# Pairing the small products on TensorE: z of eight units in four PSUM banks, reads behind scores, and placing transfers issued one by one

## The chip, the cores and the metric

The kernel runs on one core of a Trainium2 chip. The metric is the device time of one execution in microseconds (us).

## The reference, cut to what matters

Eight episodes (B = 8) have eight heads (H = 8), 512 tokens (S), 32 memory states (Ns = N) and 64 channels per head (D). Tokens read from states and states read from tokens; both results, joined along the token axis, go through a feed-forward layer with a squared relu.

```
scores  = scale * x @ state^T        a  = softmax(scores)     xread = a @ state
scores2 = scale * state @ x^T        a2 = softmax(scores2)    sread = a2 @ x
y = concat(xread, sread) as 8 * 544 rows of 512 channels
out = relu(y @ w_in)^2 @ w_out       w_in 512 x 2048, w_out 2048 x 512
```

## The kernel before, in words

**Tiling.** The 2048 hidden channels are 16 blocks of 128. A *unit* is one pair of episode and block: 8 x 16 = 128 units over the tokens (512 columns each), and 16 more over the 256 states of all episodes together. `units` (line 518) lists them in order: episode 0 blocks 0 to 3, episode 1 blocks 0 to 7, the rest of episode 0, the rest of episode 1, and then episodes 2 to 7 whole. `first_of[b]` is the number of an episode's first unit: 32 for episode 2, 48 for episode 3 and so on.

**The hidden product without xread.** The kernel doesn't form xread. As a @ state @ w_in = a @ (state @ w_in), it makes z = state @ w_in per episode and block (`z_piece`, lines 137 to 185), for four units at a time: sixteen matmul records of 64 rows x 32 columns, which lie side by side in the array. ScalarE copies z to z_hi, VectorE subtracts to z_lo, and the attention weights are held as a_hi and a_lo. A unit then is, on TensorE: six matmuls of the hidden product (`up`, line 403: z_hi and z_lo with a_hi and a_lo) and twelve of the output product (`down`, lines 442 to 460: w_out and g, each in a high and a low part). Between them, `relu` (line 406) writes r in SBUF, `square` (line 411) multiplies ph by r on VectorE and leaves the result in the PSUM bank ph, and `high` and `low` (lines 94 to 101) split it into g_hi (ScalarE) and g_lo (VectorE). The first four units (PLAIN) do without the split.

**Scores and reads.** `scores` (line 229) is again a product of 64x32 tiles; the softmax over the states (`soft`, lines 264 to 336) runs mostly on VectorE. For sread, e2 is kept and exponentiated, turned by VectorE (`turn2`, line 338), and moved to its place by sixteen DMAs on SyncE's queue (`place`, lines 345 to 352). Then `read` (lines 354 to 363) multiplies on TensorE in tiles of 128x32, `scale` (line 365) applies the sums, and `collect` (line 372) gathers on GpSimd (POOL).

**PSUM.** Of eight banks, four hold the output products (po), two the hidden products (ph, lines 400 and 70), and two form one buffer px, which z pieces, scores, reads and the turned reads share one after another (lines 71, 160, 216, 355).

**What sets the order.** Each step is registered with an engine, an estimated cost and what it needs (`add`, line 633). `Plan.run` (lines 637 to 684) plays them through and puts on each engine, among the steps ready within 0.35 us, the one with the longest remaining chain; the order that comes out is fixed in the program. On TensorE a line (lines 900 to 947) strings up n, then down n-2 and end n-2 (the second part of down), one unit after another. Visits of z, scores and reads are not on that line: the planner puts them where they are ready. A z piece waits for the px buffer and for the units that used the z buffer two chunks back (lines 837 to 839). Up n waits for g_lo of unit n-2, which frees its bank (line 904). The placing of an episode is one step on SyncE with an estimated cost of 6.0 (line 821).

```
def reads(b, px):                                                      # 816
    add(f"place{b}", SP, 6.0, my["place"], [f"late_turn.{b}", *old], LAND)          # 821
    add(f"read{b}", PE, 1.1, my["read"], [f"place{b}", f"xn{b}", *px], 0.5)         # 822
...
at = first_of[b] - (6.5 if b > 1 else 4.5 if b else 100)               # 879
at = first_of[b + 2] - 9.5 if b + 2 < B else first_of[B - 1] + 2.5 + 4 * (b + 2 - B)
```

The steps' calls in the program:

Of the kernel before, what the change touches and what calls it, by code (L numbers as in the profile page):

```python
# [19 lines left out]
def memory_attention_then_relu2_ffn(  # L20
# [116 lines left out]
    def z_piece(b, units, first, plain):  # L137

        my, own = [], []

        def banks():
            if not own:
                own.extend(ps_o.tile([P, S], F32, name=f"pz{g}", tag="po") for g in range(NG))
            return own

        z_banks[b, units[0]] = banks

        def product():
            c, at = divmod(units[0], ZC)
            if at == 0:  # L150
                zt[b, c] = [
                    sb.tile([P, NG, ZC * P], F32R, name=n, bufs=2) for n in ("z_hi", "z_lo")
                ]
            width = len(units) * P
            cols = slice(units[0] * P, units[0] * P + width)
            dst = slice(at * P, at * P + width)
            if first:
                pz = [bank[:, :width] for bank in banks()]
            else:
                both = ps_x.tile([P, NG, S], F32, name="pz", tag="px")  # L160
                pz = [both[:, g, :width] for g in range(NG)]
            for j in range(HG):
                for g in range(NG):
                    rows = slice(g * D, (g + 1) * D)
                    nc.tensor.matmul(  # L165
                        pz[g][j * N:(j + 1) * N], lhsT=state[b][rows, j, :],
                        rhs=wi[rows, j, cols], start=True, stop=True,
                    )
            z_hi, z_lo = zt[b, c]
            if plain:  # L170
                z = z_hi.bitcast(F32)
                my.extend(
                    (lambda g=g: nc.scalar.copy(out=z[:, g, dst], in_=pz[g]), None)
                    for g in range(NG)
                ) if first else my.append(
                    (lambda: nc.scalar.copy(out=z[:, :, dst], in_=both[:, :, :width]), None)
                )
            elif first:
                my.extend(
                    parts_of(z_hi[:, g, dst], z_lo[:, g, dst], pz[g], nc.vector) for g in range(NG)  # L180
                )
            else:
                my.append(parts_of(z_hi[:, :, dst], z_lo[:, :, dst], both[:, :, :width], nc.vector))

        return product, lambda: [h() for h, l in my], lambda: [l() for h, l in my]
# [3 lines left out]
    def attention(b):  # L189
# [155 lines left out]
        def place():  # L345
            my["e"] = sb.tile([P, NG, NT, HG, N], F32, name="e_t", tag="at", bufs=1)
            for j in range(HG):
                for i in range(P // N):
                    nc.sync.dma_start(  # L349
                        out=my["e"][i * N:(i + 1) * N, :, :, j, :],  # L350
                        in_=my["eq"][j * N:(j + 1) * N, :, :, i, :],
                    )

        def read():
            my["pr"] = ps_x.tile([P, NG, S], F32, name="pr", tag="px")
# [31 lines left out]
    def mlp(parts):  # L387

        todo_, gs = [], {}
# [4 lines left out]
        def up(n):  # L394
# [124 lines left out]
    first_of = [units.index((b, 0)) for b in range(B + 1)]  # L519

    sums = {}

    def batch(b, fcs):
        def first(fc):
            c, i = divmod(fc, ZC)
            f = slice(i * P, (i + 1) * P)
            z_hi, z_lo = zt[b, c]
            if b == 0 and fc < PLAIN:
                at = steps_of[b][0]["at"]()
                return [(z_hi[:, g, f].bitcast(F32), at[:, g, :]) for g in range(NG)]  # L530
            a_hi, a_lo = a_of[b]
            return [
                (w[:, g, f], v[:, g, :])
                for w, v in ((z_hi, a_hi), (z_lo, a_hi), (z_hi, a_lo))
                for g in range(NG)
            ]
# [154 lines left out]

    steps_of = [attention(b) for b in range(B)]
# [32 lines left out]
    last_z = {b: f"z{b}.{max(i for i in range(0, NFC, ZC))}.up" for b in range(B)}  # L725
# [45 lines left out]
    def softmax1(b, px):  # L771
# [3 lines left out]
        if b:  # L775
            add(
                f"scores{b}", PE, 1.3, my["scores"],
                [f"xT{b}", f"state{b}"] + (px if b > 1 else ["z0.0.high"]), 0.7,
# [37 lines left out]
    def reads(b, px):  # L816
# [4 lines left out]
        add(f"place{b}", SP, 6.0, my["place"], [f"late_turn.{b}", *old], LAND)  # L821
        add(f"read{b}", PE, 1.1, my["read"], [f"place{b}", f"xn{b}", *px], 0.5)
# [5 lines left out]
        return [f"scale{b}"]  # L828

    chunks, z_ready = [], {}  # L830

    def z_of(b, cover, first, px):
        chunk = b, cover[0] // ZC
        if chunk not in chunks:
            chunks.append(chunk)
        needs = [f"state{b}"] + [have[fc] for fc in cover]
        if len(chunks) > 2:
            ob, oc = chunks[-3]
            needs += [f"up{ob}.{fc}" for fc in range(oc * ZC, (oc + 1) * ZC)]
        alone = first < 2  # L840
        plain = b == 0 and cover[0] < PLAIN
        product, high, low = z_piece(b, cover, alone, plain)
        needs += ["idle2", "z0.0.high"] * (first == 1)
        name, width = f"z{b}.{cover[0]}.", len(cover) * NG * P
        add(name + "up", PE, 0.5 + 0.6 * width / 1024, product, needs + px * (not alone), 0.4)
        add(name + "high", ACT, act(width), high, [name + "up"])
        done = [name + "high"]
        if not plain:
            add(name + "low", DVE, dve(width), low, [name + "high"])
            done += [name + "low"]  # L850
        z_ready.update({(b, fc): done for fc in cover})
        return px if alone else done
# [13 lines left out]
    now = 0  # L866
    for n, (b, fcs) in enumerate(parts):
        i = fcs[0]
        while i <= fcs[-1]:
            width = ZC if n else 1 if i < 2 else 2  # L870
            first = now + i - fcs[0]
            pairs.append((
                first if first >= 2 else first - 2,
                lambda px, b=b, cover=range(i, i + width), first=first: z_of(b, cover, first, px),
            ))
            i += width
        now += len(fcs)
    for b in range(B):
        at = first_of[b] - (6.5 if b > 1 else 4.5 if b else 100)
        pairs.append((at, lambda px, b=b: softmax1(b, px)))  # L880
        at = first_of[b + 2] - 9.5 if b + 2 < B else first_of[B - 1] + 2.5 + 4 * (b + 2 - B)
        pairs.append((at, lambda px, b=b: reads(b, px)))
# [7 lines left out]
    bank_of = steps_of[0][0]["places"], steps_of[1][0]["places"], z_banks[0, 1]  # L890
# [9 lines left out]
    line, rows = None, []  # L900
    for n, (b, fc) in enumerate(units):
        u, width = name_of[n], blocks[segment[n]]["width"]
        product, relu, square, high, low = up(n)
        needs = [f"{'g_low' if n - 2 >= PLAIN else 'square'}{name_of[n - 2]}"] if n >= 2 else []
        if n < PLAIN:
            needs += z_ready[b, fc] + [f"back{b}.{h}" for h in range(chain_of[b])]
            cost = 8 * MM
        elif b < B:
            needs += z_ready[b, fc] + [
                f"{name}{b}.{h}" for name in ("high", "low") for h in range(chain_of[b])  # L910
            ]
            cost = 6 * MM
        else:
            w_high, w_low = weights_of(fc)
            old = [f"up{name_of[n - 2]}"] if fc >= 2 else [
                f"up{cb}.{i}" for cb, cc in chunks[-2 + fc:][:1] for i in range(cc * ZC, cc * ZC + ZC)
            ]
            add(f"w{fc}.high", ACT, act(NCC * P), w_high, old)
            add(f"w{fc}.low", DVE, dve(NCC * P), w_low, [f"w{fc}.high"])
            needs += [f"w{fc}.high", f"w{fc}.low"]  # L920
            needs += [f"reads{i}.{k}" for i in range(NGB) for k in ("high", "low")]
            cost = 12 * 0.12
        add(f"up{u}", PE, cost, product, needs, 0.25, line)
        line = f"up{u}"
        add(f"relu{u}", ACT, act(width), relu, [line] + ([f"square{name_of[n - 1]}"] if n else []))
        on = (ACT, act(width)) if n < NFC else (DVE, dve(width))
        before = [f"end{name_of[n - 2]}"] if n >= 2 else []
# [78 lines left out]
```

## Time and profile before

| What | Before |
|---|---|
| Median of 3 runs | 661.6 us (661.27 to 661.68) |
| Profiled execution | 661.63 us |
| Its span, first to last instruction | 659.8 us |
| TensorE matmul busy | 644.6 us (98%) |
| VectorE busy | 388.1 us (59%) |
| ScalarE busy | 280.1 us (42%) |
| POOL busy | 9.9 us (1%) |
| Mean granted TensorE clock | 0.999 of 2.4 GHz |

The busy times are shares of the span. Matmuls overlap, and their ends are modelled, so TensorE's busy time says that there was always one under way, not how well they fill the array. What one step adds is read from start to start.

### The profile page before, as it was taken

What the parts mean: (1) busy time and instruction counts of PE and PEld (TensorE: products, weight loads), DVE (VectorE), ACT (ScalarE), POOL (GpSimd) and SP (SyncE); (2) the same over time, 40 slices, a digit from 0 to 9 for tenths busy, and PEclk for the clock granted to TensorE, in tenths of its full rate; (3) what the DMA queues carried; (4) which work ended last, traced back from release to release, by engine and by line L of the source; (5) the groups of instructions that cost most, each with busy time, mean ns of one, the idle gap of its engine ahead of it and who ended that gap; (6) DMA issues with size and microseconds to landing.
All of it is one profiled execution on the core that took longest, in us unless ns stands there. A gap on an engine that the chain in (4) does not pass through costs nothing.

```text
span 659.8 us, 9720 instructions
## 1 busy us (share of the span) xinstructions
PE 644.6 (98%) x3844; PEld 488.4 (74%) x3844; DVE 388.1 (59%) x543; ACT 280.1 (42%) x466; POOL 9.9 (1%) x38
## 2 busy tenths in 40 slices
PE   6799999999999999999999999999999999999997
PEld 4247777777787777777777877777777787778896
DVE  6999798477535844385436744395436653443553
ACT  3767674344323533343333433353334433343542
POOL 0000000000000000000000000000000000000000
PEclk9999999999999999999999999999999999999999
DMA  8534653230212011111121011112120115000100
GB/s 318 199 129 140 212 192 135 66 132 14 84 37 81 18 29 64 65 69 31 66 66 64 17 40 44 65 65 34 64 66 0 24 33 137 2 0 1 65 1 32
DMA packets 51581, 47.81 MB, mean 72 GB/s; under 512 B 36048, under 2 KB 39376, under 8 KB 49744
## 3 DMA queue, kind: packets, MB, share of 16 engines
q1 hardware_dynamic: 51248, 47.00, 22.2%
q8 instruction: 30, 0.49, 0.3%
q10 hardware_dynamic: 288, 0.20, 0.1%
q14 instruction: 15, 0.12, 0.1%
HBM read 34.08 MB, written 8.91 MB: 65 GB/s over the span
## 4 chain that ended last, share of the span: by engine, by line
PE 90%; DVE 3%; DMA 3%; SPq 2%; issue 1%; ACT 0%; DVEq 0%
PE po L458 53%; PE ph L403 28%; PE pz L165 4%; DMA wi_raw<-w_in 3%; SPq L349 2%; PE pr L360 1%; PE po L449 1%; PE pst L234 1%; DVE a_lo L99 0%; DVE wi L122 0%; DVE wof L122 0%; DVE wof L128 0%; SPq L205 0%; DVE g_lo L99 0%; SPq L492 0%
## 5 line engine op out<-in xcount | busy, mean ns | idle before, releaser
L458 PE MATMUL po<-wo_hi,g_hi 128*128 128x512 f32 x528 | 207.2, 392 | 0.0
L458 PE MATMUL po<-wo_lo,g_hi 128*128 128x512 f32 x528 | 205.8, 390 | 0.0
L408 ACT ACTIVATE r<-ph 128x512 f32<-128x512 f32 (+1 forms) x144 | 82.6, 574 | 187.5 <-PE ph L403 187.5
L419 DVE TENSOR_TENSOR ph<-ph,r 128x512 f32<-128x512 f32 (+1 forms) x128 | 85.1, 665 | 113.1 <-ACT r L408 112.9
L458 PE MATMUL po<-wo_hi,g_lo 128*128 128x512 f32 x528 | 150.0, 395 | 0.0
L99 DVE TENSOR_TENSOR g_lo<-ph,g_hi 128x512 fp32r<-128x512 f32 (+1 forms) x140 | 91.5, 654 | 89.9 <-PE po L458 76.3
L458 PEld LDWEIGHTS po<-wo_hi,g_lo 128*128 128x128 f32 x528 | 97.3, 188 | 38.5 <-issue 19.3
L458 PEld LDWEIGHTS po<-wo_hi,g_hi 128*128 128x128 f32 x528 | 99.2, 188 | 30.8 <-ACT r L408 8.4
L96 ACT CAST g_hi<-ph 128x512 fp32r<-128x512 f32 (+1 forms) x140 | 78.9, 564 | 91.4 <-PE po L458 77.3
L458 PEld LDWEIGHTS po<-wo_lo,g_hi 128*128 128x128 f32 x528 | 99.2, 188 | 19.9
L403 PE MATMUL ph<-a_hi,z_hi 128*128 128x512 f32 x248 | 78.9, 399 | 1.0 <-DVE g_lo L99 1.0
L403 PE MATMUL ph<-a_lo,z_hi 128*128 128x512 f32 x248 | 76.8, 391 | 0.4 <-DVE a_lo L99 0.4
L403 PE MATMUL ph<-a_hi,z_lo 128*128 128x512 f32 x248 | 76.8, 391 | 0.2 <-DVE z_lo L99 0.2
L99 DVE TENSOR_TENSOR z_lo<-pz,z_hi 128x1024 fp32r<-128x1024 f32 x31 | 37.9, 1223 | 43.6 <-ACT z_hi L96 42.9
L403 PEld LDWEIGHTS ph<-a_hi,z_hi 128*128 128x128 f32 x248 | 45.6, 188 | 12.9 <-DVE g_lo L99 1.8
L403 PEld LDWEIGHTS ph<-a_lo,z_hi 128*128 128x128 f32 x248 | 46.5, 188 | 10.8 <-DVE a_lo L99 0.8
L403 PEld LDWEIGHTS ph<-a_hi,z_lo 128*128 128x128 f32 x248 | 46.5, 188 | 10.4 <-DVE z_lo L99 0.6
L96 ACT CAST z_hi<-pz 128x1024 fp32r<-128x1024 f32 x31 | 31.5, 1015 | 45.7 <-PE pz L165 45.7
L165 PE MATMUL pz<-wi,sp_raw 64*32 64x512 f32 (+2 forms) x544 | 35.3, 576 | 0.0
L375 POOL COPY sr<-rd 32x128 f32<-32x128 f32 x32 | 9.2, 287 | 551.6 <-DVE rd L367 550.5
L165 PEld LDWEIGHTS pz<-wi,sp_raw 64*32 64x32 f32 x544 | 6.3, 105 | 13.0 <-issue 7.2
L113 ACT ACTIVATE wi<-wi_raw 128x1024 f32<-128x1024 f32 (+1 forms) x9 | 9.4, 1040 | 14.0 <-DMA wi_raw<-w_in 14.0
(85 smaller groups left out, 418.8 us busy)
## 6 DMA issues: line engine op xcount, KB each, us to landing
wo_raw<-w_out SPq DMA_DIRECT2D x8, 1024.0 KB, 5.0
xn_raw<-xn SPq DMA_DIRECT2D x8, 1024.0 KB, 5.5
out<-sum SPq DMA_DIRECT2D x32, 256.0 KB, 2.3
xt_raw<-xT SPq DMA_DIRECT2D x7, 1024.0 KB, 5.3
wi_raw<-w_in SPq DMA_DIRECT2D x7, 1024.0 KB, 4.8
e_t<-eq SPq DMA_DIRECT2D x128, 32.0 KB, 1.9
wi_raw<-w_in SPq DMA_DIRECT2D x2, 512.0 KB, 5.7
xt_raw<-xT SPq DMA_DIRECT2D x2, 512.0 KB, 6.0
```

Source lines behind the costliest of these rows:

```text
L96: nc.scalar.copy(out=hi, in_=src)
L99: eng_lo.tensor_sub(out=lo, in0=src, in1=hi.bitcast(F32))
L113: nc.scalar.activation(out_f, high.bitcast(F32), AF.Abs, scale=2.0**-112)
L165: nc.tensor.matmul(pz[g][j * N:(j + 1) * N], lhsT=state[b][rows, j, :], rhs=wi[rows, j, cols], start=True, stop=True,)
L234: nc.tensor.matmul(place[g][j * N:(j + 1) * N], lhsT=state[b][rows, j, :], rhs=my["t"][rows, j, own], start=True, stop=True,)
L349: nc.sync.dma_start(out=my["e"][i * N:(i + 1) * N, :, :, j, :], in_=my["eq"][j * N:(j + 1) * N, :, :, i, :],)
L360: nc.tensor.matmul(my["pr"][j * N:(j + 1) * N, g, :D], lhsT=my["e"][:, g, t, j, :], rhs=my["n"][:, t, h * D:(h + 1) * D], start=t == 0, st ...
L375: nc.gpsimd.tensor_copy(out=sr[b // GB][at:at + N, j * NG * D:(j + 1) * NG * D], in_=my["rd"][j * N:(j + 1) * N].rearrange("p g d -> p (g ...
L403: nc.tensor.matmul(ph, lhsT=w, rhs=v, start=m == 0, stop=m == len(todo) - 1)
L408: nc.scalar.activation(r, my[0], AF.Relu)
L419: nc.vector.tensor_mul(out=ph, in0=ph, in1=r)
L458: nc.tensor.matmul(po[t], lhsT=g, rhs=w, start=i == 0 and j == 0, stop=i == last and j == 2)
```

## The change

**z.** From unit 32 on, a chunk of four units is one of a pair. The pair stands on TensorE's line at a *slot*: ahead of up n-6, if n is the pair's first unit. Its first piece takes the two ph banks (one for each half of the heads, evacuated by two copies and two subtractions), its second the px buffer. In such a slot, down n-2 and end n-2 (n here the slot's unit) come ahead of up n. z is kept as unit by half by column, and half of the z chunks lie in the buffers that had held the raw weights (tag `raw`), so a chunk waits for the units four chunks back, not two.

**Scores and reads.** From episode 2 on, the scores of episode b stand on the line ahead of up `first_of[b] - 10`, and the reads of episode b-2 right behind them. The reads of the last two episodes stand ahead of units 117 and 121. Reads use one ph bank in place of px.

**Relu and square.** From unit 24 on (`kept_from`), r has three buffers and the square is r * r in SBUF. The bank ph is free after the relu; up n waits for the relu of unit n-2. In every unit, whatever stands in the slot takes its bank in the same turn.

**Placing** is sixteen steps of 0.65 in the planner, one for each DMA, in a row but with others between them where the planner sees fit.

The diff, cut:

```diff
+    def z_tiles(k):
+        if k not in zt and in_raw(k):
+            both = sb.tile([P, 2, ZC, NG, P], F32R, name="z_both", tag="raw", bufs=RAW)
+            zt[k] = [both[:, 0], both[:, 1]]
+        if k not in zt:
+            zt[k] = [sb.tile([P, ZC, NG, P], F32R, name=n, bufs=2) for n in ("z_hi", "z_lo")]
+        return zt[k]
...
+            if not own and home == "px":
+                both = ps_x.tile([P, NG, S], F32, name="pz", tag="px")
+                own.extend(both[:, g] for g in range(NG))
+                own.append(both)
+            elif not own:
+                pool = dict(po=ps_o, ph=ps_h)[home]
+                own.extend(pool.tile([P, S], F32, name=f"pz{g}", tag=home) for g in range(NG))
...
-        def place():
-            my["e"] = sb.tile([P, NG, NT, HG, N], F32, name="e_t", tag="at", bufs=1)
-            for j in range(HG):
-                for i in range(P // N):
...
+        def place(k):
+            j, i = divmod(k, P // N)
...
-            my["pr"] = ps_x.tile([P, NG, S], F32, name="pr", tag="px")
+            my["pr"] = ps_h.tile([P, NG, S // NG], F32, name="pr", tag="ph")
...
-                r = sb.tile([P, S], F32, name="r", bufs=1)[:, :width]
+                if n < kept_from or n % 3 == 0:
+                    r = sb.tile([P, S], F32, name="r", bufs=1)[:, :width]
+                else:
+                    if not r_late:
+                        r_late.append(sb.tile([P, 2, S], F32, name="r_late", tag="wof", bufs=1))
+                    r = r_late[0][:, n % 3 - 1, :width]
...
+                if n >= kept_from:
+                    nc.vector.tensor_mul(out=r, in0=r, in1=r)
+                    my[0] = r
+                    return
...
+    late_from = first_of[2]
+    kept_from = late_from - 8
+    def in_raw(k):
+        return k * ZC >= late_from and k % 4 < 2
...
+    pieces = [(0, 1, "po", None), (1, 1, "po", None), (2, 2, "px", None)]
+    pieces += [(n, ZC, "px", None) for n in range(PLAIN, late_from, ZC)]
+    for n in range(late_from, first_of[B], 2 * ZC):
+        pieces += [(n, ZC, "ph", n - 6), (n + ZC, ZC, "px", n - 6)]
...
-                f"scores{b}", PE, 1.3, my["scores"],
+                f"scores{b}", PE, 1.1, my["scores"],
...
+    def in_slot(n, name, free=()):
+        before = slots.setdefault(n, [])
+        line = before[-1][0] if before else f"end{name_of[n - 3]}"
+        before.append((name, free))
+        return line
...
-        add(f"place{b}", SP, 6.0, my["place"], [f"late_turn.{b}", *old], LAND)
-        add(f"read{b}", PE, 1.1, my["read"], [f"place{b}", f"xn{b}", *px], 0.5)
+        for k in range(HG * P // N):
+            add(
+                f"place{b}.{k}", SP, 0.65, lambda k=k: my["place"](k),
+                [f"late_turn.{b}", *old], LAND, f"place{b}.{k - 1}" if k else None,
+            )
...
+            f"read{b}", PE, 0.9, my["read"], [f"place{b}", f"xn{b}"], 0.3,
+            in_slot(slot, f"read{b}", [[f"scale{b}"]]),
...
-        add(name + "up", PE, 0.5 + 0.6 * width / 1024, product, needs + px * (not alone), 0.4)
...
+            name + "up", PE, 0.24 * (home == "ph" or not slot) + 0.86 * count / ZC, product, needs + px * (home == "px"), 0.4,
+            in_slot(slot, name + "up", frees * (home == "ph")) if slot else None,
...
+        slot = first_of[b] - 10 if b > 1 else None
...
+        if b > 1:
+            pairs.append((slot + 0.1, lambda px, b=b, slot=slot: reads(b - 2, slot) or px))
+    for b, slot in (B - 2, first_of[B - 1] + 5), (B - 1, first_of[B - 1] + 9):
+        pairs.append((slot, lambda px, b=b, slot=slot: reads(b, slot) or px))
...
+        for name, frees in slots.get(n, []):
+            line = name
+            for free in frees:
+                plan.steps[name][4].update(ph_free[-2])
+                ph_free.append(free)
+        todo = range(max(0, n - 2), n - 1 if n + 1 < len(units) else n + 1)
+        early_downs = any(len(frees) > 1 for _, frees in slots.get(n, []))
+        if early_downs:
+            downs(todo)
+        needs = [*ph_free[-2]]
+        ph_free.append([f"{'relu' if n >= kept_from else 'g_low' if n >= PLAIN else 'square'}{u}"])
...
+        if n >= kept_from:
+            old += [f"g_low{name_of[n - 3 if n - 3 >= kept_from else n - 1]}", f"wo{NK - 1}.low"]
+        add(f"relu{u}", ACT, act(width), relu, [line, *old])
```

## Rows read from the trace of the kernel before

**Rows 1.** Page, busy us (share of the span) and instructions of each engine.

```profile
PE 644.6 (98%) x3844; PEld 488.4 (74%) x3844; DVE 388.1 (59%) x543; ACT 280.1 (42%) x466; POOL 9.9 (1%) x38
```

**Rows 2.** Chain in order of time, 110 to 150 us: start us, us, what.

```profile
131.35 1.36 PE ph L403 x6
...
135.43 1.36 PE ph L403 x6
136.79 1.02 PE pst L234 x16
...
140.77 1.36 PE ph L403 x6
...
146.11 1.36 PE ph L403 x6
```

**Rows 3.** Timeline of TensorE, a z visit: start us, us, line, operation, records.

```profile
141.74 0.39 PE L403 MATMUL ph<-a_lo,z_hi 128*128 128x512 f32 x1
142.06 0.66 PE L165 MATMUL pz<-wi,sp_raw 64*32 64x512 f32 x8
...
142.51 0.64 PE L165 MATMUL pz<-wi,sp_raw 64*32 64x512 f32 x8
...
143.08 0.50 PE L458 MATMUL po<-wo_hi,g_hi 128*128 128x512 f32 x1
143.41 0.39 PE L458 MATMUL po<-wo_lo,g_hi 128*128 128x512 f32 x1
```

**Rows 4.** The same chain as rows 2, around a visit of reads.

```profile
120.67 1.03 PE pr L360 x64
121.70 1.58 PE ph L403 x6
```

**Rows 5.** Timeline of SyncE's queue: start us, us to issue, count.

```profile
61.06 11.67 SPq L349 DMA_DIRECT2D e_t<-eq  x16
72.84 0.53 SPq L492 DMA_DIRECT2D wi_raw<-w_in  x1
...
541.18 10.78 SPq L349 DMA_DIRECT2D e_t<-eq  x16
552.00 0.60 SPq L211 DMA_DIRECT2D xn_raw<-xn  x1
```

**Rows 6.** Timeline of TensorE, 78.7 to 86 us, with [idle before <-releaser].

```profile
80.50 0.73 PE L403 MATMUL ph<-a_hi,z_hi 128*128 128x512 f32 x2 [0.63 <-DVE g_lo L99]
81.07 0.62 PE L403 MATMUL ph<-a_hi,z_lo 128*128 128x512 f32 x2
...
85.23 0.73 PE L403 MATMUL ph<-a_hi,z_hi 128*128 128x512 f32 x2 [0.36 <-DVE g_lo L99]
```

**Rows 7.** Groups by line: count, busy us, mean ns, idle before, releasers.

```profile
L419 DVE TENSOR_TENSOR ph<-ph,r 128x512 f32<-128x512 f32 x112 | 78.2, 698 | 93.1 <-ACT r L408 92.9
...
L96 ACT CAST g_hi<-ph 128x512 fp32r<-128x512 f32 x124 | 73.0, 588 | 88.9 <-PE po L458 76.4 <-DVE ph L419 10.9 <-PE po L449 1.6
...
L99 DVE TENSOR_TENSOR z_lo<-pz,z_hi 128x1024 fp32r<-128x1024 f32 x31 | 37.9, 1223 | 43.6 <-ACT z_hi L96 42.9
...
L96 ACT CAST z_hi<-pz 128x1024 fp32r<-128x1024 f32 x31 | 31.5, 1015 | 45.7 <-PE pz L165 45.7
...
L99 DVE TENSOR_TENSOR wi_lo<-wi,wi_hi 128x512 fp32r<-128x512 f32 x16 | 11.1, 691 | 1.1
...
L96 ACT CAST wi_hi<-wi 128x512 fp32r<-128x512 f32 x16 | 9.8, 612 | 0.0
```

**Rows 8.** Busy us, 140 to 160 us: PE, PEld, DVE, ACT, POOL.

```profile
140.00:160.00 20.00, 20.00 (x101) 15.61 (x99) 18.59 (x26) 10.41 (x19) 0.00 (x0) 1.00 0.26 100
```

**Rows 9.** Timeline of all engines, 508 to 511 us, around a z visit.

```profile
508.04 1.09 PE L165 MATMUL pz<-wi,sp_raw 64*32 64x512 f32 x16
...
509.23 1.02 ACT L96 CAST z_hi<-pz 128x1024 fp32r<-128x1024 f32 x1 [1.30 <-PE pz L165]
...
510.28 1.23 DVE L99 TENSOR_TENSOR z_lo<-pz,z_hi 128x1024 fp32r<-128x1024 f32 x1
```

More of the change, by code (lines that the diff above doesn't have):

```diff
@@ L135, in memory_attention_then_relu2_ffn, with z_piece @@
     zt, z_banks = {}, {}
-    def z_piece(b, units, first, plain):
+    def z_tiles(k):
[5 more added lines that the diff above has]
+        return zt[k]
+    def z_piece(n, units, home, plain):
         my, own = [], []
+        b, fc = units[0]
+        width = len(units) * P
+        cols = slice(fc * P, fc * P + width)
         def banks():
-            if not own:
-                own.extend(ps_o.tile([P, S], F32, name=f"pz{g}", tag="po") for g in range(NG))
+            if not own and home == "px":
[5 more added lines that the diff above has]
+                own.extend(pool.tile([P, S], F32, name=f"pz{g}", tag=home) for g in range(NG))
             return own
-        z_banks[b, units[0]] = banks
+        z_banks[n] = banks
         def product():
[L149 to L161, printed above, removed]
+            pz = banks()
             for j in range(HG):
@@ L165, in product @@
                     nc.tensor.matmul(
-                        pz[g][j * N:(j + 1) * N], lhsT=state[b][rows, j, :],
+                        pz[g][j * N:(j + 1) * N, :width], lhsT=state[b][rows, j, :],
                         rhs=wi[rows, j, cols], start=True, stop=True,
                     )
[L169 to L181, printed above, removed]
-            else:
-                my.append(parts_of(z_hi[:, :, dst], z_lo[:, :, dst], both[:, :, :width], nc.vector))
-        return product, lambda: [h() for h, l in my], lambda: [l() for h, l in my]
+            z_hi, z_lo = (z[:, n % ZC:n % ZC + len(units)] for z in z_tiles(n // ZC))
+            if home == "px":
+                todo = [(slice(0, NG), pz[NG][:, :, :width].rearrange("p g (u f) -> p u g f", f=P))]
+            else:
+                todo = [(g, pz[g][:, :width].rearrange("p (u f) -> p u f", f=P)) for g in range(NG)]
+            for g, src in todo:
+                if plain:
+                    z = z_hi.bitcast(F32)[:, :, g]
+                    my.append((lambda z=z, src=src: nc.scalar.copy(out=z, in_=src), None))
+                else:
+                    my.append(parts_of(z_hi[:, :, g], z_lo[:, :, g], src, nc.vector))
+        moves = 1 if home == "px" else NG
+        return product, [[lambda i=i, k=k: my[i][k]() for k in range(2)] for i in range(moves)]
     state = {}
@@ L519, in memory_attention_then_relu2_ffn @@
     first_of = [units.index((b, 0)) for b in range(B + 1)]
+    at_of = {u: n for n, u in enumerate(units)}
+    late_from = first_of[2]
+    kept_from = late_from - 8
+    def in_raw(k):
+        return k * ZC >= late_from and k % 4 < 2
     sums = {}
@@ L776, in softmax1 @@
             add(
-                f"scores{b}", PE, 1.3, my["scores"],
-                [f"xT{b}", f"state{b}"] + (px if b > 1 else ["z0.0.high"]), 0.7,
+                f"scores{b}", PE, 1.1, my["scores"],
+                [f"xT{b}", f"state{b}"] + (px if b > 1 else ["z0.0.high0", "z0.0.high1"]), 0.7,
+                in_slot(slot, f"scores{b}") if slot else None,
             )
@@ L814, in memory_attention_then_relu2_ffn, with reads @@
     last_up = [max(n for n, u in enumerate(units) if u[0] == b) for b in range(B)]
-    def reads(b, px):
+    slots = {}
+    def in_slot(n, name, free=()):
[3 more added lines that the diff above has]
+        return line
+    def reads(b, slot):
         my = steps_of[b][0]
@@ L827, in reads @@
         add(f"collect{b}", POOL, 1.3, my["collect"], [f"scale{b}"])
[L828 to L844, printed above, removed]
-        add(name + "up", PE, 0.5 + 0.6 * width / 1024, product, needs + px * (not alone), 0.4)
[L846 to L852, printed above, removed]
+    z_ready = {}
@@ new lines, in z_of @@
+    def z_of(n, count, home, slot, px):
+        cover = units[n:n + count]
+        b, fc = cover[0]
+        k = n // ZC
+        needs = [f"state{b}"] + [have[fc] for _, fc in cover]
+        if n >= late_from and k < late_from // ZC + 2:
+            needs += [f"wo{NK - 1}.low"]
+        elif k > 1:
+            old = k - (4 if k * ZC > late_from else 2)
+            needs += [f"up{name_of[m]}" for m in range(old * ZC, (old + 1) * ZC)]
+        plain = n < PLAIN
+        product, moves = z_piece(n, cover, home, plain)
+        needs += ["idle2", "z0.0.high0", "z0.0.high1"] * (n == 1)
+        name, size = f"z{b}.{fc}.", count * NG * P // len(moves)
+        frees = []
+        for i, (high, low) in enumerate(moves):
+            done = [f"{name}high{i}"]
+            add(done[0], ACT, act(size), high, [name + "up"])
+            if not plain:
+                done += [f"{name}low{i}"]
+                add(done[1], DVE, dve(size), low, done[:1])
+            frees.append(done)
+        add(
+            name + "up", PE, 0.24 * (home == "ph" or not slot) + 0.86 * count / ZC, product, needs + px * (home == "px"), 0.4,
+            in_slot(slot, name + "up", frees * (home == "ph")) if slot else None,
+        )
+        z_ready.update({u: sum(frees, []) for u in cover})
+        return sum(frees, []) if home == "px" else px
@@ L864, in reads_turned @@
         return [name + "high", name + "low"]
[L866 to L877, printed above, removed]
-    for b in range(B):
[L879 to L882, printed above, removed]
+    for n, count, home, slot in pieces:
+        pairs.append((
+            slot or (n if n >= 2 else n - 2),
+            lambda px, n=n, count=count, home=home, slot=slot: z_of(n, count, home, slot, px),
+        ))
+    for b in range(B):
+        slot = first_of[b] - 10 if b > 1 else None
+        pairs.append((
+            slot or first_of[b] - (4.5 if b else 100),
+            lambda px, b=b, slot=slot: softmax1(b, px, slot),
+        ))
+        if b > 1:
+            pairs.append((slot + 0.1, lambda px, b=b, slot=slot: reads(b - 2, slot) or px))
+    for b, slot in (B - 2, first_of[B - 1] + 5), (B - 1, first_of[B - 1] + 9):
+        pairs.append((slot, lambda px, b=b, slot=slot: reads(b, slot) or px))
     for i in range(NGB):
@@ L897, in memory_attention_then_relu2_ffn, with downs @@
         )
[L900 to L927, printed above, removed]
-        add(f"square{u}", *on, square, [f"relu{u}"] + (before if n < PLAIN else []))
-        if n >= PLAIN:
-            add(f"g_high{u}", ACT, act(width), high, [f"square{u}"] + before)
-            add(f"g_low{u}", DVE, dve(width), low, [f"g_high{u}"])
-        for m in range(max(0, n - 2), n - 1 if n + 1 < len(units) else n + 1):
+    line, rows, ph_free = None, [], [[], []]
+    def downs(todo):
+        nonlocal line, rows
+        for m in todo:
             u, fc = name_of[m], units[m][1]
```

64 lines of the change are left out of this document (51 added, 13 removed).

## The prediction, made blind

> **What bounds the kernel now.** I read the page's busy times first [rows 1]: TensorE 98% of the span, VectorE 59%, ScalarE 42%. Then the chain that ended last, in order of time [rows 2], to see what a plain unit costs on TensorE and what a visit of another product adds. From one hidden product to the next, a plain unit takes 135.43 - 131.35 = 4.08 us. With the second scores in it: 140.77 - 135.43 = 5.34. With a z piece: 146.11 - 140.77 = 5.34. So a visit costs 1.26 us. A visit of the reads costs 1.03 plus 0.22, by which the hidden product after it is longer than 1.36: 1.25 us [rows 2, 4]. TensorE is what sets the end; a microsecond taken from its stream is one off the span, as long as nothing else then makes it wait.
>
> What is in those 1.26 us shows in the single records [rows 3]. The last 128x128 matmul before the visit starts at 141.74; at its usual pitch (4.08 us for 18, so 0.227) the next start would be 141.97, but z begins at 142.06: 0.09 lost going in. Sixteen records run as eight and eight, 0.45 apart. The second eight start at 142.51; after another 0.45 one would go on at 142.96, but the next starts at 143.08, and the one after it 0.33 later instead of 0.23: 0.22 lost coming out. With some hundredths in the records behind, 1.26 is about 0.90 of streaming and 0.36 of change of tile shape, in and out.
>
> **The change, part by part.** The sum is made against the profiled execution, 661.63 us, whose span is 659.8; it stands 0.03 above the median of the three runs, so no correction is needed.
>
> (a) *Twelve pairs of z pieces.* From unit 32 on, the 24 pieces of four units stand as twelve pairs, the second right behind the first, same tile shape, in banks of its own. The second should cost its streaming, 0.90, in place of 1.26: 0.36 saved. Ends: 0, if every piece pays its own change of shape as the visits alone do, and 0.40, if it costs the 0.86 that the changed planner writes for a second piece (an estimate in the code). I take 0.36, because eight records follow eight at 0.45 within one piece, which is the nearest row. 12 x 0.36 = **4.3 us** (0 to 4.8).
>
> (b) *Six reads behind scores.* Reads 0 to 5 move right behind scores 2 to 7; reads 6 and 7 stay alone. The two have different tile shapes, 64x32 and 128x32, and no row shows a step from one to the other. Ends: 0, if it costs both an exit and an entry, and 0.36, if it costs neither. The nearest rows are the changes to and from 128x128, 0.09 in and 0.22 out; with one change of that size, their mean, left between the two, 0.36 - 0.16 = 0.20 is saved. 6 x 0.20 = **1.2 us** (0 to 2.2). What hangs on the reads moves with them at no cost: the scale on VectorE, four copies on POOL (POOL is busy 1% of the span, [rows 1]) and on SyncE the next xn load, which has some 16 units until its own read. The Trainium skill, TensorEngine Tiling (Array Packing), section Key Properties, says that a change of the tiling mode drains TensorE while a change of tile inside one mode does not. By it (a) stands, and (b) would stand nearer its lower end, the whole about half a microsecond less; no run here yet shows that step.
>
> (c) *Placing as sixteen steps.* The sixteen placing DMAs of episode 0 held SyncE's queue from 61.06 for 11.67 us as one step, where the planner reckoned with 6.0. The load of the next w_in slab was issued behind them at 72.84 [rows 5]. ScalarE converts that slab ahead of the next g_hi, and the bank that g_lo frees came late: TensorE waited for g_lo twice, 0.63 and 0.36 us, and the first two matmuls after each wait took 0.73 instead of the usual 0.62 [rows 6]: 1.2 us. With steps of 0.65 us the planner can put the load in front. Sixteen placings, late loads, xn loads and output stores now share the queue step by step; the placing itself ends later, but read 0 moves to slot 22, tens of microseconds after it. I take **1.0 us** (0 to 1.5, since the two stretches also lose some tenths that the rows put down to modelled ends).
>
> (d) *Two hidden banks lent to z.* In twelve slots, eight units apart, the first piece takes both hidden banks. It waits for the relu of the two units before, not for their g_lo: the square now stays in SBUF. Behind it on TensorE stand the px piece (0.90), down and end of unit n-2 (12 of the 18 matmuls of 4.08, so 2.72) and then up n, which needs the first bank back: 3.6 us. To free it, ScalarE copies half a piece and VectorE subtracts it, by the rows of 512 elements about 0.59 and 0.69 [rows 7]: 1.3 us if both engines come at once. 2.3 us to spare, so nothing. Up n+1, which needs the second bank, stands another 1.36 us (the other 6 of 18) behind. Reads take one hidden bank until their scale, and up n runs in the other; nothing. If that cover is gone, up n waits (third rival).
>
> (e) *Relu and square in SBUF.* g_hi read from SBUF should cost what wi_hi does, 612 ns instead of 588, the square what wi_lo does, 691 against 698 [rows 7]. Two halves instead of a whole piece add 0.16 us on either engine (2 x 588 - 1015, 2 x 691 - 1223), twelve times. Both lie beside TensorE's stream: nothing. The relu's new wait, for g_lo three units back, holds ScalarE's g_hi and z_hi behind it, but that g_lo is over two units earlier: nothing. If VectorE falls behind, these too count (second rival).
>
> (f) *Start and end.* The startup's work up to unit 3 and the sixteen state units keep their instructions; 0, between -0.5 and +0.5. Read 7 needs read 6, then SyncE's placing, which held the queue 10.78 us, and the xn load behind it [rows 5]; four plain units between the two reads give 16.3 us, enough if the load is put among the placings: 0 (up to 2 lost).
>
> Sum: 661.63 - 4.3 - 1.2 - 1.0 = **655.1 us**.
>
> **Rivals.** *Second: VectorE is full around slots 22 to 28.* There the scores of episode 2 come earlier than now (before unit 22; the old place was 6.5 units ahead of unit 32), and with them the softmax chain. The adds into episode 0's sums, the z of unit 24, the first pair and the z of unit 28 follow, the z pieces linked by the one px buffer. VectorE is at 18.59 of 20 us there already [rows 8]. Unit 28's z can start only when the pair's second piece is out of px, and must itself be copied and split within some 9 us: 1.0 + 1.2 for the pair's piece, 1.26, and 1.0 + 1.2 again, 5.7 us without any other work. Two operations of 1.22 us in the way use most of it up. Price about 2 us, once: 657. Against: at that load TensorE is busy for all 20 us of the stretch now.
>
> *Third, slower: the lent banks come back late.* It decides in each of the twelve pair slots, at up n. If VectorE has three operations on 1024 elements ahead of the first z_lo, at the 1.22 us that z_lo takes on as many [rows 7], that is 3.66 against 2.3 to spare: 1.3 us lost, twelve times 1.3 = 16: 671. It breaks even at 6.5 / 12 = 0.54 us per pair, that is with 2.85 us of other work ahead. Against: in the fullest stretch late in the run, z ended at 509.13, z_hi began at 509.23 and z_lo at 510.28, 0.03 after z_hi's end [rows 9]; the planner puts z_lo first when it is due. For: the slot two units into a new episode also has its output rows' copies on both engines.
>
> *Fourth: each piece pays its change of shape anyway.* Then (a) and most of (b) vanish: 661.63 - 1.0 - 1.2 = 659.4. For: no row shows two pieces back to back. Against: eight and eight at 0.45.
>
> *Fifth: it doesn't do what it says* (the early wait returns elsewhere, and the pairs bring little): 660.5 to 662.
>
> **How the numbers follow.** Forecast 0.58, with its own range 653.0 to 656.5 from the ends of (a) to (c) that lie near; second 0.18; third 0.08; fourth 0.08; fifth 0.08. The range 653.0 to 659.5 leaves out the third, the fifth and little else. A measurement of this kernel tells 0.2% (1.3 us) from no change. Faster: 0.58 + 0.18 + 0.08 + some of the fifth = 0.86; the rest of the fifth within 0.2%, 0.06; slower 0.08.
>
> **What would show it.** In the chain, pairs of z in one stretch of about 1.9 us and a unit with a pair 2.16 longer than 4.08, not 2.5; scores and reads 2.3 together, not 2.5. No wait of TensorE near 80 and 85 us. Matmul rows of the hidden product with no idle before them in slots 26, 34, 42 and so on. Wrong would be idle there that ended with z_lo, a wait around units 26 to 28, or thirty-two z records that pause 0.3 us in their middle.

## The result and the profile after

The changed kernel takes 653.18 us, median of four runs (652.95 to 653.65), against 661.43 for the kernel before (661.19 to 661.68): 0.9872 of its time, 95% interval 0.9859 to 0.9884. That is 8.25 us, 1.2%, faster. The profiled execution took 652.97 us, 8.66 less than the one before. 655.1 was forecast: the direction is right, and the median lies at the very bottom of the range, whose lower end, 653.0, the profiled execution just misses. The gain was sized 6.5.

The page's first part, busy time of each engine with its share of the span and its instructions, for the changed kernel:

```profile
PE 637.5 (98%) x3844; PEld 491.4 (75%) x3844; DVE 388.3 (60%) x555; ACT 286.2 (44%) x478; POOL 10.7 (2%) x38
```

TensorE's matmul busy time falls by 7.1 us with the same 3844 instructions; VectorE's stays, and ScalarE's rises by 6 us, which its idle time swallows [rows 1]. The chain in order of time (start us, us, what), around a pair of z pieces and around scores with reads:

```profile
242.32 1.36 PE ph L404 x6
...
246.40 1.88 PE pz L169 x32
248.28 2.94 PE po L468 x12
251.22 2.72 PE ph L404 x12
...
260.74 1.36 PE ph L404 x6
...
264.82 1.02 PE pst L235 x16
265.84 1.03 PE pr L361 x64
266.87 1.58 PE ph L404 x6
...
271.18 0.91 PE ph L404 x4
```

From 242.32 to 251.22 lie a hidden product, two output products and the pair: 8.90 us, of which 6 + 24 matmuls are 6.80. The pair costs **2.10** us, two visits of before 2.52 [rows 2]. From 260.74 to 271.18 lie two plain units (8.16) and scores with reads: **2.28** us, where before they cost 1.26 + 1.25 = 2.51.

The timeline of TensorE inside a pair's visit (start us, us, line, operation, records), the answers for several short windows one below the other, so that the second eight of the first piece show as 246.78 and those of the second as 247.64:

```profile
246.01 0.39 PE L468 MATMUL po<-wo_hi,g_lo 128*128 128x512 f32 x1
246.33 0.66 PE L169 MATMUL pz<-wi,sp_raw 64*32 64x512 f32 x8
...
246.78 0.64 PE L169 MATMUL pz<-wi,sp_raw 64*32 64x512 f32 x8
...
247.21 1.06 PE L169 MATMUL pz<-wi,sp_raw 64*32 64x512 f32 x16
...
247.64 0.64 PE L169 MATMUL pz<-wi,sp_raw 64*32 64x512 f32 x8
248.21 0.50 PE L468 MATMUL po<-wo_hi,g_hi 128*128 128x512 f32 x1
248.54 0.40 PE L468 MATMUL po<-wo_lo,g_hi 128*128 128x512 f32 x1
```

Eights follow at 0.45, 0.43 and 0.43 us. Nothing stands between the two pieces: the second takes 0.86. Going in costs 0.09 as before, and coming out 248.21 - 247.64 - 0.43 = 0.14 and another 0.10 to the next matmul.

With the starts of single units the whole difference falls into place. They are read from the timelines of TensorE (us from the span's start).

| Profile | Unit 4 | Unit 18 | Unit 22 | Unit 118 | Unit 122 | First state unit | From unit 4 to there |
|---|---|---|---|---|---|---|---|
| Before | 36.81 | 102.93 | 121.63 | 560.23 | 578.79 | 604.65 | 567.84 |
| Changed | 36.44 | 101.05 | 120.78 | 552.98 | 570.55 | 596.00 | 559.56 |
| Changed, once more | 36.86 | 101.45 | 121.17 | 553.46 | 571.03 | 596.48 | 559.62 |
| Unpaired | 37.38 | 101.98 | 121.70 | 558.50 | 576.07 | 601.52 | 564.14 |
| Reads apart | 37.05 | 101.65 | 120.34 | 555.68 | 573.25 | 598.70 | 561.65 |
| Reads first | 36.75 | 101.31 | 121.04 | 553.19 | 570.76 | 596.21 | 559.46 |
| z twice | 36.90 | 101.47 | 121.19 | 563.77 | 581.50 | 606.95 | 570.05 |
| Square in PSUM | 39.20 | 103.29 | 123.01 | 569.16 | 586.74 | 611.71 | 572.51 |
| Placing whole, 6.0 | 37.94 | 103.40 | 123.12 | 555.32 | 573.51 | 598.96 | 561.02 |
| Placing whole, 10.4 | 36.55 | 101.08 | 120.81 | 553.07 | 571.18 | 596.62 | 560.07 |
| Before, with steps | 37.04 | 101.65 | 120.35 | 558.60 | 577.16 | 603.02 | 565.98 |
| Before, square in SBUF | 37.05 | 103.11 | 121.81 | 560.06 | 578.62 | 604.48 | 567.43 |

Up to unit 4 each engine runs the same steps in the same order in all twelve profiles, so the differences in that column belong to no edit. In ten of them unit 4 starts 18.13 to 18.17 us behind the landing of the third load of w_in, which came between 18.3 and 19.2 us. In the other two (square in PSUM; placing whole, 6.0) it starts 1.5 us later than that. There TensorE's granted clock was 0.71 and 0.50, and 0.51 and 0.64, in the two stretches of 2 us from 26 to 30, the lower of its two levels (1.2 and 2.4 GHz) for all or part of each; in the changed kernel it was 1.00 in both. Just before, TensorE had stood 1.67 and 1.66 us waiting for z_hi, but it did so in the changed kernel too (1.66), so why the clock fell in these two is not shown. The column on the right doesn't hang on the start, so the parts are compared there. The changed kernel's two profiles agree in it within 0.06 us.

### The profile page after: what moved, and what is told of

Its sections match the earlier page's. It is cut to its first block, busy times and chain, and to the rows that moved or that the text cites. A ratio compares the mean times of both kernels' runs of the same rounds, so it can differ in the third digit from the quotient of the medians.

```text
span 651.2 us, 9536 instructions
## 1 busy us (share of the span) xinstructions
PE 637.5 (98%) x3844; PEld 491.4 (75%) x3844; DVE 388.3 (60%) x555; ACT 286.2 (44%) x478; POOL 10.7 (2%) x38
## 4 chain that ended last, share of the span: by engine, by line
PE 93%; DVE 3%; DMA 2%; SPq 1%; issue 0%; ACT 0%; DVEq 0%
PE po L468 56%; PE ph L404 30%; PE pz L169 4%; DMA wi_raw<-w_in 2%; PE pr L361 1%; PE po L459 1%; PE pst L235 1%; DVE a_lo L99 0%; DVE wof L122 0%; DVE wof L128 0%; SPq L206 0%; SPq L502 0%; DVE q L290 0%; DVE at L276 0%; DVE q L317 0%
## 5 line engine op out<-in xcount | busy, mean ns | idle before, releaser
L420 DVE TENSOR_TENSOR r_late<-r_late 128x512 f32<-128x512 f32 (+1 forms) x80 | 52.2, 653 | 67.7 <-ACT r_late L414 67.6
L99 DVE TENSOR_TENSOR g_lo<-r_late,g_hi 128x512 fp32r<-128x512 f32 (+1 forms) x80 | 52.0, 650 | 67.5 <-PE po L468 57.6
L414 ACT ACTIVATE r_late<-ph 128x512 f32<-128x512 f32 (+1 forms) x80 | 45.4, 568 | 98.0 <-PE ph L404 97.7
L96 ACT CAST g_hi<-r_late 128x512 fp32r<-128x512 f32 (+1 forms) x80 | 47.4, 592 | 74.7 <-PE po L468 53.8
L414 ACT ACTIVATE r<-ph 128x512 f32<-128x512 f32 (+1 forms) x64 | 37.2, 581 | 64.5 <-PE ph L404 64.2
L404 PE MATMUL ph<-a_hi,z_both 128*128 128x512 f32 x192 | 52.1, 393 | 0.0
L404 PE MATMUL ph<-a_hi,z_hi 128*128 128x512 f32 x152 | 48.3, 399 | 0.0
L404 PE MATMUL ph<-a_lo,z_hi 128*128 128x512 f32 x152 | 47.0, 390 | 0.4 <-DVE a_lo L99 0.4
L404 PE MATMUL ph<-a_hi,z_lo 128*128 128x512 f32 x152 | 47.0, 390 | 0.3 <-DVE z_lo L99 0.3
L404 PEld LDWEIGHTS ph<-a_hi,z_both 128*128 128x128 f32 x192 | 35.6, 188 | 7.6
```

Source lines behind the costliest of these rows:

```text
L96: nc.scalar.copy(out=hi, in_=src)
L99: eng_lo.tensor_sub(out=lo, in0=src, in1=hi.bitcast(F32))
L404: nc.tensor.matmul(ph, lhsT=w, rhs=v, start=m == 0, stop=m == len(todo) - 1)
L420: nc.vector.tensor_mul(out=r, in0=r, in1=r)
```

## Experiments

The kernel before ran beside each set of kernels, at medians of 661.40 to 661.94 us. In the first sets the parts stood 0.3 to 1.9 us further above the changed kernel than the units' starts explain, so the changed kernel was run again beside the last set.

**Control: the changed kernel once more.**

> The changed kernel once more, unchanged, for the comparisons with the parts. From the start of unit 4 to the first state unit it took 559.6 us, the kernel before 567.8. Theory: 653.2 us, and the same 559.6; the start up to unit 4, which has differed by up to a microsecond between profiles, is where any difference lies. Rival (the single parts' runs were about a microsecond slower because of what they changed): it comes out at 653.2 with an unchanged start.

653.89 us (653.47 to 654.55), 0.9886 of before (0.987 to 0.9903). From unit 4 to the states it took 559.62. The start is where profiles differ.

**The pairs taken apart.**

```diff
-pieces += [(n, ZC, "ph", n - 6), (n + ZC, ZC, "px", n - 6)]
+pieces += [(n, ZC, "ph", n - 6), (n + ZC, ZC, "px", n - (4 if n > late_from else 6))]
```

> The second piece of eleven of the twelve pairs stands two units later, as a visit of its own; the first pair stays. Theory (a pair saves one change of tile shape): in the changed kernel's records the second piece costs 0.86 us and a unit with a pair is 2.10 us longer, a visit alone 1.26, so this should cost 11 x 0.42 = 4.6 us: 657.8 us. Rival 1 (the gain comes from the lent banks, the earlier release and the fixed order, not from standing together): 653 us. Rival 2 (0.36 per pair, as the prediction had it): 657.1 us; told from the theory by the units' lengths.

658.52 us, 0.9951 of before (0.9938 to 0.9964). Chain of this kernel, in order of time:

```profile
244.09 1.36 PE ph L404 x6
...
248.17 1.02 PE pz L169 x16
...
252.15 2.72 PE ph L404 x12
...
257.59 1.02 PE pz L169 x16
258.61 1.58 PE ph L404 x6
```

The first piece's visit, at 248.17, adds 252.15 - 244.09 - 6.80 = 1.26, the second's, at 257.59, again 1.02 and the longer hidden product. In total 564.14 - 559.56 = 4.58 us dearer, 0.416 for each of eleven pairs. The theory holds, and rival 1 falls: the lent banks and the early release are the changed kernel's, every visit has its fixed place on the line, and the gain of the eleven pairs is gone.

**One piece of a pair multiplied twice.**

```diff
-            for j in range(HG):
+            for j in [*range(HG)] * (2 if home == "ph" else 1):
```

> The first piece of each of the twelve pairs is multiplied twice into the same banks, sixteen more records in each pair's visit, same tile shape. Theory (a further piece in a visit costs its streaming alone, 0.43 us for each eight records): 12 x 0.86 = 10.3 us dearer, 663.5 us. Rival (each piece pays a change of shape): 12 x 1.26 = 15.1, 668.3 us. Rival of the prediction (0.90 a piece): 664.0 us; told apart by the records' pitch of 0.43 or 0.45 us.

664.01 us, 1.0045 of before (1.003 to 1.0059). The visit in the chain:

```profile
249.41 2.74 PE pz L169 x48
```

Forty-eight records take 2.74 us where thirty-two take 1.88: 0.86 for sixteen more. From unit 4 on it is 570.05 - 559.56 = 10.49 us, of which 0.16 belongs to longer last reads, between units 118 and 122 (17.73 us against 17.57). That leaves 10.33, 0.86 a piece; neither 1.26 nor 0.90 fits. The median alone could not tell 0.86 from 0.90: it stands 10.8 us above the changed kernel's first median and 10.1 above its second.

**Reads apart from scores, and in the other order.**

```diff
-pairs.append((slot + 0.1, lambda px, b=b, slot=slot: reads(b - 2, slot) or px))
+pairs.append((slot + 2, lambda px, b=b, slot=slot + 2: reads(b - 2, slot) or px))   # apart
+pairs.append((slot - 0.1, lambda px, b=b, slot=slot: reads(b - 2, slot) or px))     # reads first
```

> The reads of episodes 0 to 5 stand two units behind the scores instead of right behind them. Theory (scores and reads together save part of one change of shape, 0.23 us by the units' lengths, 2.28 against 2.51): 6 x 0.23 = 1.4 us dearer, 654.6 us. Rival (the step from 64x32 to 128x32 costs as much as an exit and an entry, and the gain was elsewhere): 653.2 us, no change. Second rival (no cost at all in that step): 6 x 0.36 = 2.2, 655.4 us.

655.67 us, 0.9909 of before (0.9895 to 0.9924); from unit 4 on 2.09 us dearer than the changed kernel, not 1.4. Five of the six separations cost 0.23 each: behind unit 25, which starts at 135.96 here and at 134.41 in the changed kernel, unit 118 is 1.15 us later than that difference gives. The sixth came with a wait, which the list of TensorE's waits shows (engine, line, waited for: us, times, longest):

```profile
PE ph L404 <- DVE g_lo L99: 0.6, 1, 0.6
```

It stands ahead of unit 24, where this order puts g_lo late. So the theory's 0.23 holds, and the other 0.7 us belong to that wait and the slower matmuls right behind it, which came with the other order and are no price of the change of shape.

> Reads stand right ahead of the scores in the same slot, so the step is from 128x32 to 64x32. Theory (a change between two tile shapes drains the array once, in either direction): 2.28 us for the two as now, 653.2 us. Rival (the step costs less or nothing that way, since the last reads are short): 0.1 to 0.14 less each, six times, at most 0.8 us faster, seen only in the units' starts.

653.16 us, 0.9872 of before (0.9857 to 0.9887). Chain:

```profile
261.00 1.36 PE ph L404 x6
...
265.08 1.03 PE pr L361 x64
266.11 1.02 PE pst L235 x16
267.13 1.58 PE ph L404 x6
...
271.44 1.36 PE ph L404 x6
```

271.44 - 261.00 - 8.16 = 2.28 us again, and 559.46 from unit 4 on. A change between 64x32 and 128x32 costs the same either way; the rival falls.

**Relu and square as before, with the banks lent.**

```diff
-    kept_from = late_from - 8
+    kept_from = len(units)
```

> Everything as changed, but relu and square as before: one r buffer, the square left in the PSUM bank, which is free only after g_lo. Theory (lending both hidden banks needs the early release): the first piece of a pair then waits for g_lo of the unit just before. Its g_hi starts when end n-3 ends, so TensorE stands for g_hi 0.59 and g_lo 0.65 us, about 1.3 us, in each of twelve slots: 15.6 us, 669 us, with TensorE waiting for g_lo at z. The reads need only one bank and should not wait. Rival (the banks would come back in time anyway, and the move to SBUF is neutral): 653 us.

667.18 us, 1.0078 of before (1.0065 to 1.0092): slower than the kernel before, and 12.95 us slower than the changed one from unit 4 on, 1.1 us per pair. Chain ahead of one pair:

```profile
249.39 2.51 PE po L468 x11
...
251.93 0.59 ACT g_hi L96
...
252.54 0.70 DVE g_lo L99
...
253.29 1.95 PE pz L169 x30
```

TensorE's output product ends at 251.90; then g_hi and g_lo run one after the other, and only then most of the z records. Two of thirty-two had started in the first bank. That is the loss the slower rival of the prediction feared, in the slots it named but by another wait: the first piece waits for its banks, not up n behind it. The profiled execution, the slowest of the five at 668.70 us, lost another 2.3 to 2.8 us before unit 4. That isn't the edit's: the third load of w_in landed at 19.57 us, against 18.28 in the changed kernel, and the rest is the lower clock before 30 us.

**The placing in one step, with two estimates.**

```diff
-        for k in range(HG * P // N):
-            add(
-                f"place{b}.{k}", SP, 0.65, lambda k=k: my["place"](k),
...
+        add(
+            f"place{b}", SP, 6.0, lambda: [my["place"](k) for k in range(HG * P // N)],
+            [f"late_turn.{b}", *old], LAND,
+        )
```

The second kernel has 10.4 in place of 6.0.

> The placing is again one step of sixteen DMAs, with the old estimate of 6.0; all else as changed. Theory (the steps let the load of the next weights go in between, which took away two waits of TensorE near 80 and 85 us, 1.6 us in the starts of the units): 1.6 us dearer, 654.8 us, and TensorE waits again before 90 us. Rival (the order of the start changed for another reason, and the waits stay away): 653.2 us.

656.55 us, 0.992 of before (0.9906 to 0.9933). From unit 4 on 1.46 us dearer, 0.85 of them up to unit 18 and 0.62 from unit 118 to 122; the start up to unit 4 came out 1.1 later than in the control, which is the lower clock before 30 us. The median lies 2.66 above the control's; whether the clock fell there too in the runs that were not profiled is not known. ScalarE's and TensorE's timelines (with [idle before <-releaser]):

```profile
78.59 1.12 ACT L113 ACTIVATE wi<-wi_raw 128x1024 f32<-128x1024 f32 x1 [3.55 <-DMA wi_raw<-w_in]
79.61 0.58 ACT L96 CAST g_hi<-ph 128x512 fp32r<-128x512 f32 x1
...
80.97 0.72 PE L404 MATMUL ph<-a_hi,z_hi 128*128 128x512 f32 x2 [0.40 <-DVE g_lo L99]
...
85.70 0.73 PE L404 MATMUL ph<-a_hi,z_hi 128*128 128x512 f32 x2 [0.34 <-DVE g_lo L99]
```

The waits of before are back. ScalarE stands 3.55 us before the conversion of a weights slab, with g_hi behind it, and TensorE waits for the g_lo after that.

> The placing as one step of sixteen DMAs, but with an estimate of 10.4 instead of 6.0. Theory (the steps matter, not the estimate, since SyncE is free and no load ready when the placing is): as with one step of 6.0, TensorE waits for g_lo before 90 us and units 8 to 18 take about 1.3 us longer than in the changed kernel: 654.6 us. Rival (the wrong estimate was the fault): 653.2 us and no such wait.

654.02 us, 0.989 of before (0.9872 to 0.9908). The rival was right: with an honest estimate the early waits are gone, although SyncE is held just as long and the load goes out just as late. SyncE's and ScalarE's timelines:

```profile
60.82 11.76 SPq L350 DMA_DIRECT2D e_t<-eq  x16
72.69 0.53 SPq L502 DMA_DIRECT2D wi_raw<-w_in  x1
...
74.69 0.59 ACT L96 CAST g_hi<-ph 128x512 fp32r<-128x512 f32 x1 [0.64 <-PE po L468]
78.38 1.12 ACT L113 ACTIVATE wi<-wi_raw 128x1024 f32<-128x1024 f32 x1 [3.10 <-DMA wi_raw<-w_in]
```

Here g_hi runs at 74.69, ahead of the conversion that waits 3.10 us for the slab, and TensorE no longer waits for g_lo there. So the late load costs TensorE nothing where ScalarE's order reckons with it. The changed kernel gets rid of the wait by the other way. Its load goes out at 65.55, and ScalarE still converts the slab ahead of g_hi, as in the kernel before, but without idle time:

```profile
73.96 1.13 ACT L113 ACTIVATE wi<-wi_raw 128x1024 f32<-128x1024 f32 x1
74.99 0.58 ACT L96 CAST g_hi<-ph 128x512 fp32r<-128x512 f32 x1
```

Either is enough: the load ahead of most of the placing, or an estimate that lets the planner put g_hi first. What the steps do have to themselves is at the end: 18.11 us from unit 118 to 122, against 17.57 in the changed kernel, and 18.19 in the other kernel with one step. SyncE's queue and the chain in the kernel with 10.4:

```profile
548.99 10.91 SPq L350 DMA_DIRECT2D e_t<-eq  x16
559.94 0.60 SPq L212 DMA_DIRECT2D xn_raw<-xn  x1
...
565.47 1.54 PE pr L361 x64
```

The load of the last xn goes out behind all sixteen placings and lands 5.2 us later, at 565.2, shortly before the last reads begin at 565.40; they take 1.54 us instead of 1.03. In the changed kernel it goes out behind twelve and lands at 563.9, and the next load of weights after seven in the first placing:

```profile
60.75 4.69 SPq L350 DMA_DIRECT2D e_t<-eq  x7
65.55 0.53 SPq L502 DMA_DIRECT2D wi_raw<-w_in  x1
...
548.90 8.44 SPq L350 DMA_DIRECT2D e_t<-eq  x12
557.39 0.60 SPq L212 DMA_DIRECT2D xn_raw<-xn  x1
```

**Single parts on the kernel before.** One has the placing as sixteen steps, the other r and the square in SBUF from unit 24 on with the bank free after the relu; both by the lines of the change.

> The kernel before with one part alone: the placing as sixteen steps of 0.65 in the planner. Theory: the load of the next weights goes in between, TensorE's waits near 80 and 85 us go, 1.6 us: 659.9 us, and the reads of episode 7 may lose the 0.35 us by which they were longer than the others (659.5). Rival (with reads not moved, the placing of episode 0 is as urgent as the load and nothing moves): 661.4 us.

660.11 us, 0.9978 of before (0.9969 to 0.9986). To unit 18 it takes 64.61 us from unit 4, as the changed kernel does and not 66.12; from unit 4 to the states it is 1.86 us faster. Of these, 1.51 are the early waits and 0.35 the last reads, which took 1.38 us in the kernel before and 1.03 here.

> The kernel before with one part alone: from unit 24 on three buffers for r, the square in SBUF, and a hidden bank free after the relu. Theory (TensorE never waited for a hidden bank there, so the early release is worth nothing by itself): 661.4 us within 0.5. Rival (it does help by itself, with freer ScalarE and VectorE order): below 660 us. Other rival (SBUF reads are dearer and show): above 662.5 us.

661.44 us, 0.9997 of before (0.9988 to 1.0005). The early release and the move to SBUF are worth nothing alone. Its last reads took 1.03 us too, with the placing whole: the 0.35 of before lie at the edge. The xn load landed 0.65 us ahead of those reads here and 0.32 ahead of them in the kernel before.

## Where the prediction was right, and the step that failed

**What bounds the kernel** held: TensorE's stream sets the end, and the whole difference is in what it runs or waits for. Against the terms:

| Term | Forecast | Measured |
|---|---|---|
| (a) twelve pairs | 4.3 | 5.0 (12 x 0.42) |
| (b) six reads behind scores | 1.2 | 1.4 (6 x 0.23) |
| (c) early waits | 1.0 | 1.5 |
| (f) last reads | 0 | 0.35 |
| start up to unit 4, chance | 0 | 0.37 |
| Sum | 6.5 | 8.6 |

The forecast of 655.1 us was 2.1 us too high for the profiled execution. Terms (a) to (c) as measured make 661.63 - 7.9 = 653.7 us, still inside the range; the last reads and the start, for which its lower end left no room, carry the profiled execution just below it. The start is chance: the third load of w_in landed at 18.67 us before and at 18.28 in the changed kernel.

**(a) is the step that failed by most: the price of a pair's second piece was too high.** "The second should cost its streaming, 0.90": I took the 0.45 between the two eights of one piece as the pitch. It is 0.45 only for the first step of a visit, 0.43 for every one after it, so the second piece costs 0.86, and a pair saves 0.42 us, not 0.36: 0.7 us in twelve pairs. The upper end, 0.40, left out another 0.02. It lies in the matmuls behind the visit, whose next 24 steps take 5.59 us behind a lone piece and 5.57 behind a pair; why is not shown. The pair experiment and the doubled piece bear the prices out, so the fourth rival (each piece pays its change of shape) is out. Its own figure, 659.4, took off all of (b), of which its sentence keeps a part; without (b) it would have been 660.6.

**(b)** was right in kind: one change stays between the two. TensorE's timeline of the changed kernel, the last eight records of the scores and the first of the reads:

```profile
265.20 0.64 PE L235 MATMUL pst<-xt_raw,sp_raw 64*32 64x512 f32 x8
265.77 0.32 PE L361 MATMUL pr<-xn_raw,e_t 128*32 128x64 f32 x8
```

Between them lie 0.57 us, 0.14 more than the pitch of 0.43. That is as much as the first step from z back to 128x128 loses, and 0.23 is saved in all, not 0.20. The rule of the Trainium skill, TensorEngine Tiling (Array Packing), section Key Properties, that only a change of the mode drains TensorE, agrees with both: 0.14 between scores and reads, 0 between two pieces. I had let it speak for the lower end; the trace puts (b) above the middle.

**(c)** had the right mechanism and too low a price. The rows gave 1.2 and the starts of units give 1.5; I cut it to 1.0 for no row. In the changed kernel the wait goes as forecast, with the load put among the placings. What the forecast didn't see is that this is not the only way: a right estimate takes the wait away too, with the load as late as before.

**(d)** held. In a pair's slot ScalarE and VectorE free the first bank early:

```profile
247.51 1.07 ACT L96 CAST z_hi<-pz 128x512 fp32r<-128x512 f32 x2 [0.48 <-PE pz L169]
...
248.13 1.29 DVE L99 TENSOR_TENSOR z_lo<-pz,z_hi 128x512 fp32r<-128x512 f32 x2 [1.68 <-ACT z_hi L96]
```

The first z_lo of the two that begin at 248.13 is done by 248.8. The next hidden product begins at 251.06 by TensorE's timeline, so 2.3 us are to spare, as forecast:

```profile
251.06 0.61 PE L404 MATMUL ph<-a_hi,z_both 128*128 128x512 f32 x2
```

The relu's earlier release, which (d) took for granted, is what it rests on, as the experiment with the square in PSUM shows. The third, slower rival, VectorE busy ahead of the first z_lo, didn't come.

**(e)** held. From SBUF g_hi takes 622 ns (612 were forecast, 588 from PSUM), and the square 690 (691 forecast, 698 in PSUM) [rows 7]:

```profile
L420 DVE TENSOR_TENSOR r_late<-r_late 128x512 f32<-128x512 f32 x69 | 47.6, 690 | 65.8 <-ACT r_late L414 65.7
...
L96 ACT CAST g_hi<-r_late 128x512 fp32r<-128x512 f32 x69 | 42.9, 622 | 65.7 <-PE po L468 51.7 <-DVE r_late L420 14.0
```

**The second rival** (VectorE full around units 22 to 28) had its condition but not its price. In the windows (columns as in [rows 8]) VectorE has 29.14 - 9.94 = 19.20 of 20 us from 120 to 140, and TensorE waits for nothing:

```profile
120.00:160.00 40.00, 40.00 (x278) 29.95 (x268) 29.14 (x41) 18.30 (x30) 1.14 (x4) 1.00 0.32 95
140.00:160.00 20.00, 20.00 (x113) 15.24 (x98) 9.94 (x15) 7.91 (x13) 0.00 (x0) 1.00 0.29 77
```

From unit 25 to unit 29, with the first pair and one more piece, it took 154.09 - 134.41 = 19.68 us, and 4 x 4.08 + 2.10 + 1.26 is 19.68.

**(f)** named the last reads, with "enough if the load is put among the placings"; it missed that the kernel before already paid there, 1.38 us for those reads against 1.03 for others [rows 4]. The row stands in the chain of the kernel before, but not in the prediction's sum:

```profile
558.93 1.38 PE pr L360 x64
```

## What to carry to other kernels

Where a tuned kernel's matmul engine never stops, look at what small products cost beyond their records: with 0.40 us around each visit, two that stand together in one tile shape save it once, and the room for that (banks, and an earlier release of them) is worth preparing though it brings nothing alone. Give a planner true costs before moving work about: an estimate of 6.0 for a step that held its queue for 11.7 us had ordered another engine's queue so that the busiest one waited, and 10.4 in its place was enough to end that. When a price comes from the first step of a repeated pattern, ask whether later steps pay it too.

## What the runs showed that was not expected

A visit of z records (eights of 64x32 tiles, 512 columns) has its first step at 0.45 us and all others at 0.43. A placing that holds SyncE's queue for 11.8 us near the start costs TensorE nothing if ScalarE's queue was ordered for it, while the last one still costs 0.5 us at the end. And the last reads take 1.38 and 1.54 us, not 1.03, in two profiles where their load landed 0.2 to 0.3 us before they began. No list shows this as a wait, only the comparison of like groups does. What holds up the single reads is not shown.
